# Attention, a gated mixture and a routed mixture on one core: the third weight's products of blocks 3 to 8 taken two slices at a time

## The chip, the core and the metric

The kernel runs on 1 core of one Trainium2 chip. The metric is device time in microseconds of one execution; the median of three runs of the kernel before is 960.69 us (960.13 to 963.97).

## The reference

Three layers follow each other. An attention with a local window of 32 and 32 global tokens gives 2176 rows of 512. A gated layer follows, then a routed layer of eight experts with a capacity:

```
x   = attention(q, k, v)                     # 4 x 8 heads, 512 + 32 rows, 64 wide
g   = x @ w_gate;  val = x @ w_val           # 512 -> 1536
x   = (g * sigmoid(g) * val) @ w_out         # 1536 -> 512, all of it float32
log = x @ moe2_w_gate                        # 8 logits a row; tokens assigned greedily by rank, 272 an expert
out = relu(x[mask_e] @ w1[e]) @ w2[e]        # for each expert e
```

## The kernel before, in words

The gated layer is what the change touches (the kernel calls it the first mixture). Its rows are nine **blocks** `k` = 0 to 8: blocks 0 to 7 have 256 rows, block 8 has the 128 global rows. The 1536 inner columns are twelve **slices** `f` of 128.

*One slice of one block.* `gates(f)` (line 564) multiplies the gate and the value weights with the block's inputs: 24 products in 16 bit, 12 for each half of a bank `G`. Each float32 factor is held as a high and a low part (`xth`, `xtl`; `wp` holds both parts of the weights), and three of the four combinations are added. There are two banks `G`, so slice `f + 2` writes the bank of slice `f`. After the 24 products ACT takes a tanh (L569), DVE makes `(tanh + 1) * g` (L571) and the slice's factor `th` (L573, the last reader of the bank), ACT rounds it to its high part `hh` (L576), and POOL subtracts for the low part `hl` (L578). There are three buffers of each of `hh` and `hl`.

`out(f)` (line 588) then adds the slice's product with the third weight to the block's result: `hh` with `oh` and `ol`, and `hl` with `oh`, for each of the block's two tiles of 128 rows. That is 6 products of 512 columns in a 4-byte type (3 in block 8), with `hh` and `hl` as the weights that PE loads. After slice 11, `x_rows` copies the result (`xr`, L500), and the logits follow: 8 products a tile on DVE (L523, `junk<-xr,w2gt`), put behind the gates of the next block by `logits`.

*The order of the work.* Blocks 0 to 2 run while the weights come in (`first_blocks`). `moe_block` runs blocks 3 to 8. For each slice it issues the gates, then the product of the slice before:

```
        for f in range(NF):
            yield from m.gates(f)
            ...
            if f:
                m.out(f - 1)
```

Between its pieces (`yield`) the attention of the next block is issued, piece by piece (`attn`, `globs`, `x0_t`); it ends with the transposes of L432 and the two halves `xth` (L434) and `xtl` (L435), without which the next block's gates don't go on. Blocks 5 to 8 also have the global rows' attention (`glob`, lines 443 to 480, with the split `vcl` on L307). The written order is only a wish: a planner sorts each engine's instructions by a simulated timeline before the kernel is built. `tc.add_manual_dep(..., NS, ...)` gives it a dependency that fixes an order in that timeline and makes no semaphore.

Of the kernel before, what the change touches and what calls it, by code (L numbers as in the profile page):

```python
# [13 lines left out]
OP = mybir.AluOpType  # L14
# [5 lines left out]
NF = FF // 128  # L20
# [13 lines left out]
def body(ctx, tc, units, gk, gv, wts, w2g, w1, w2, cst, cst2, out):  # L34
    nc = tc.nc
    gp, sy = nc.gpsimd, nc.sync
    NS, SY = (mybir.DependencyInfo(c, mybir.DependencyReason.DATA)
              for c in (mybir.DependencyClass.NoSync, mybir.DependencyClass.Sync))
# [19 lines left out]
    ve, sc, te = nc.vector, nc.scalar, nc.tensor  # L58
# [16 lines left out]
    def mark(ins):  # L75

        TURN[:] = [ins]
# [10 lines left out]
    def psb(tag):  # L88

        return ps.tile([128, 512], F32, name=tag, tag=tag, bufs=2 if tag == "G" else 1)  # L90
# [102 lines left out]
    def g_tile():  # L193

        return GN.pop() if GN else psb("G").rearrange("p (j t) -> p j t", j=2)
# [301 lines left out]
    def x_rows(c, px, tag):  # L497

        xr = wk.tile([128, DM], F32, name="xr", bufs=2)
        sc.activation(xr, px, AF.Copy)  # L500
        if c < 16:
            r0 = (c // 4) * 544 + 32 + 128 * (c % 4)
            sy.dma_start(xs[r0:r0 + 128, :], xr)
        else:
            sy.dma_start(xs.rearrange("(b s) d -> b s d", b=B)[:, :32, :], xr)
        if 2 * NB <= c < NT - 1:
            for e in range(NE):
                LT.append((c, e, xr))
            return
        pt = psb(tag).rearrange("p (c q) -> p c q", c=4)  # L510
        for d in range(4):
            te.transpose(pt[:, d, :], xr[:, 128 * d:128 * d + 128], ident)
        xt = wk.tile([128, 544], F32, name="pg", tag="sm")[:, :DM].rearrange("p (d t) -> p d t", d=4)
        XT_LAST[:] = [sc.activation(xt, pt, AF.Copy)]
        pl = psb(tag)
        for d in range(4):
            te.matmul(pl[:, :NE], xt[:, d], w2gc[:, d], start=(d == 0), stop=(d == 3))
        ve.tensor_copy(L[:, c], pl[:, :NE])

    def logits(n):  # L520
        for _ in range(min(n, len(LT)) if w2gt is not None else 0):
            c, e, xr = LT.pop(0)
            ve.scalar_tensor_tensor(junk[:, :DM], xr, 1.0, w2gt[:, e], op0=OP.mult, op1=OP.mult,  # L523
                                    accum_out=L[:, c, e:e + 1])

    HH = {}
# [3 lines left out]
    class Moe:  # L530
# [24 lines left out]
        def gates(self, f):  # L555
            self.scales(f)
            n, (xh, xl), ib = self.n, self.x, self.ib
            pg = g_tile()
            for j in range(2):
                i = 0  # L560
                for d in range(4):
                    o = slice(128 * d, 128 * d + 128)
                    for a, x in ((0, xh), (0, xl), (1, xh)):
                        te.matmul(pg[:, j, :n], wp_[:, f, j, a, o], x[:, d, :n], start=(i == 0), stop=(i == 11))  # L564
                        i += 1
                if j == 0:
                    yield
            th = wk.tile([128, 256], F32, name="th")
            TH[:] = [sc.activation(th[:, :n], pg[:, 0, :n], AF.Tanh, scale=ib[:, 0, f:f + 1])]  # L569
            t = th  # L570
            ve.scalar_tensor_tensor(t[:, :n], th[:, :n], 1.0, pg[:, 0, :n], op0=OP.add, op1=OP.mult)  # L571
            h = th
            mark(ve.scalar_tensor_tensor(h[:, :n], t[:, :n], ib[:, 1, f:f + 1], pg[:, 1, :n],  # L573
                                         op0=OP.mult, op1=OP.mult))
            hh = wk.tile([128, 256], F32R, name="hh", bufs=3)
            sc.activation(hh[:, :n], h[:, :n], AF.Copy)  # L576
            hl = wk.tile([128, 256], F32R, name="hl", bufs=3)
            gp.tensor_tensor(hl[:, :n], h[:, :n], hh[:, :n], op=OP.subtract)  # L578
            HH[self.k, f] = (hh, hl)

        def out(self, f):
            nt = self.n // 128
            if f == 0:
                self.px = [psb(self.tags[t]) for t in range(nt)]
            hh, hl = HH.pop((self.k, f))
            for i, (a, w) in enumerate(((hh, oh), (hh, ol), (hl, oh))):
                for t in range(nt):
                    te.matmul(self.px[t], a[:, 128 * t:128 * t + 128], w[:, f, :], start=(f == 0 and i == 0),  # L588
                              stop=(f == NF - 1 and i == 2))
            if f == NF - 1:  # L590
                for t in range(nt):
                    x_rows(2 * self.k + t, self.px[t], self.tags[t] if self.k < NB else "PTa")
# [26 lines left out]
    def moe_block(k):  # L619
        m = Moe(k)  # L620
        for f in range(NF):
            yield from m.gates(f)
            logits(f % 2)
            yield
            if f:
                m.out(f - 1)
            logits(1)
            yield
        yield
        m.out(NF - 1)  # L630


# [692 lines left out]
```

## Time and profile before

| | |
|---|---|
| median of 3 runs | 960.69 us |
| the profiled execution, its time | 965.33 us |
| its span, first to last instruction | 963.6 us |
| mean granted clock of TensorE | 0.951 |
| PE busy | 871.9 us (90%) |
| weight loads (PEld), beside PE | 732.3 us (76%) |
| DVE busy | 611.1 us (63%) |
| ACT busy | 453.0 us (47%) |
| POOL busy | 371.9 us (39%) |

The profiled execution is 4.64 us above the median. Times in the profile are microseconds from the span's start. In a timeline row the first number is the start, the second the duration; a matmul's duration holds its way through the array, so what a product costs is read from the distance between starts. A bracket gives the idle time of the engine ahead of the instruction and what ended it. The clock is the share of full speed that TensorE was granted. Blocks 3 to 8 run from 275 to 652 us; the routing and the experts follow.

### The profile page before, as it was taken

What the parts mean: (1) busy time and instruction counts of PE and PEld (TensorE: products, weight loads), DVE (VectorE), ACT (ScalarE), POOL (GpSimd) and SP (SyncE); (2) the same over time, 40 slices, a digit from 0 to 9 for tenths busy, and PEclk for the clock granted to TensorE, in tenths of its full rate; (3) what the DMA queues carried; (4) which work ended last, traced back from release to release, by engine and by line L of the source; (5) the groups of instructions that cost most, each with busy time, mean ns of one, the idle gap of its engine ahead of it and who ended that gap; (6) DMA issues with size and microseconds to landing.
All of it is one profiled execution on the core that took longest, in us unless ns stands there. A gap on an engine that the chain in (4) does not pass through costs nothing.

```text
span 963.6 us, 19509 instructions
## 1 busy us (share of the span) xinstructions
PE 871.9 (90%) x7556; PEld 732.3 (76%) x7556; DVE 611.1 (63%) x1859; ACT 453.0 (47%) x923; POOL 371.9 (39%) x344
## 2 busy tenths in 40 slices
PE   5677699999999999989979989996789989999996
PEld 4566578777788887778758757783488988999996
DVE  3677699999328579597595484268666766763210
ACT  4656454555247465445354333230554364545531
POOL 2444333444212222113111111121666786687841
PEclk8889889999999999989989999997789999999998
DMA  9631243542212233303221020001454455446600
GB/s 373 254 121 45 86 155 132 160 161 66 88 66 93 85 103 108 118 29 109 82 78 56 27 74 1 1 23 43 169 184 142 133 185 188 135 149 215 197 28 26
DMA packets 28497, 108.10 MB, mean 112 GB/s; under 512 B 3572, under 2 KB 3572, under 8 KB 28276
## 3 DMA queue, kind: packets, MB, share of 16 engines
q1 hardware_dynamic: 25332, 97.94, 30.0%
q0 software_dynamic: 3072, 8.92, 2.6%
q8 instruction: 59, 0.97, 0.4%
q14 instruction: 34, 0.28, 0.1%
HBM read 97.92 MB, written 8.91 MB: 111 GB/s over the span
## 4 chain that ended last, share of the span: by engine, by line
PE 68%; DVE 12%; issue 7%; DMA 5%; POOL 4%; ACT 3%; SPq 0%; POOLq 0%; ACTq 0%; DVEq 0%
PE G L564 26%; PE X L588 11%; PE A L1152 7%; PE A L1136 5%; PE rt L961 2%; DMA er<-w 2%; DMA xg<-xs,idx 2%; DVE junk L523 2%; DVE ge L948 1%; POOL wp L50 1%; PE PV L476 1%; PE PV L399 1%; POOL vl L50 1%; PE T L1101 1%; DMA gkr<-gv 1%
## 5 line engine op out<-in xcount | busy, mean ns | idle before, releaser
L564 PEld LDWEIGHTS <-wp 128*128 128x128 f16 x2592 | 231.6, 99 | 80.5 <-issue 52.0
L564 PE MATMUL G<-xth,wp 128*128 128x256 f16 (+1 forms) x1344 | 235.8, 270 | 4.1 <-ACT xth L434 2.5
L578 POOL TENSOR_TENSOR hl<-th,hh 128x256 fp32r<-128x256 f32 (+1 forms) x108 | 85.5, 792 | 348.1 <-ACT hh L576 274.8
L564 PE MATMUL G<-xtl,wp 128*128 128x256 f16 (+1 forms) x672 | 177.5, 270 | 4.3 <-DVE xtl L435 4.3
L1083 POOL TENSOR_TENSOR el<-er,eh 128x1024 fp32r<-128x1024 f32 x62 | 146.3, 2390 | 40.7 <-ACT eh L1080 40.4
L569 ACT ACTIVATE th<-G,ib 128x256 f32<-128x256 f32 (+1 forms) x108 | 49.4, 459 | 107.8 <-PE G L564 97.0
L571 DVE SCALAR_TENSOR_TENSOR th<-th,G 128x256 f32<-128x256 f32 (+1 forms) x108 | 43.4, 402 | 81.9 <-ACT th L569 81.0
L1080 ACT ACTIVATE eh<-er 128x1024 fp32r<-128x1024 f32 x64 | 65.5, 1054 | 49.4 <-DMA er<-w 43.2
L576 ACT ACTIVATE hh<-th 128x256 fp32r<-128x256 f32 (+1 forms) x108 | 43.4, 402 | 75.4 <-DVE th L573 75.1
L1136 PE MATMUL A<-xh,eh 128*128 128x272 f32 x256 | 77.9, 304 | 0.0
L1152 PE MATMUL A<-fh,eh 128*128 128x272 f32 x256 | 76.6, 302 | 0.0
L1136 PE MATMUL A<-xh,el 128*128 128x272 f32 x256 | 75.2, 294 | 0.0
L1136 PE MATMUL A<-xl,eh 128*128 128x272 f32 x256 | 74.9, 293 | 0.0
L1152 PE MATMUL A<-fh,el 128*128 128x272 f32 x256 | 74.4, 292 | 0.0
L1152 PE MATMUL A<-fl,eh 128*128 128x272 f32 x256 | 74.2, 291 | 0.0
L1141 DVE SCALAR_TENSOR_TENSOR fl<-A,fh 128x272 fp32r<-128x272 f32 x64 | 28.0, 439 | 59.2 <-ACT fh L1140 57.4
L523 DVE SCALAR_TENSOR_TENSOR junk<-xr,w2gt 128x512 f16<-128x512 f32 x80 | 59.0, 737 | 4.1 <-ACT xr L500 3.4
L588 PE MATMUL X<-oh,hh 128*128 128x512 f32 x156 | 57.7, 444 | 2.1 <-ACT hh L576 2.1
L588 PE MATMUL X<-oh,hl 128*128 128x512 f32 x156 | 55.7, 428 | 0.0
L573 DVE SCALAR_TENSOR_TENSOR th<-th,ib,G 128x256 f32<-128x256 f32 (+1 forms) x108 | 50.1, 464 | 2.9
L588 PE MATMUL X<-ol,hh 128*128 128x512 f32 x156 | 51.5, 403 | 0.0
L1136 PEld LDWEIGHTS A<-xl,eh 128*128 128x128 f32 x256 | 49.2, 192 | 0.1
(389 smaller groups left out, 2126.7 us busy)
## 6 DMA issues: line engine op xcount, KB each, us to landing
er<-w SPq DMA_DIRECT2D x64, 512.0 KB, 5.2
wr<-wts SPq DMA_DIRECT2D x36, 512.0 KB, 3.6
unit<-units SPq DMA_DIRECT2D x22, 688.0 KB, 4.0
unit<-gv SPq DMA_DIRECT2D x12, 640.0 KB, 3.8
wp<-units SPq DMA_DIRECT2D x10, 688.0 KB, 7.8
gkr<-gk SPq DMA_DIRECT2D x8, 608.0 KB, 4.7
xs<-xr SPq DMA_DIRECT2D x17, 256.0 KB, 2.0
gkr<-gv SPq DMA_DIRECT2D x4, 640.0 KB, 7.3
```

Of the source, the lines that this page charges most:

```text
L523: ve.scalar_tensor_tensor(junk[:, :DM], xr, 1.0, w2gt[:, e], op0=OP.mult, op1=OP.mult, accum_out=L[:, c, e:e + 1])
L564: te.matmul(pg[:, j, :n], wp_[:, f, j, a, o], x[:, d, :n], start=(i == 0), stop=(i == 11))
L569: TH[:] = [sc.activation(th[:, :n], pg[:, 0, :n], AF.Tanh, scale=ib[:, 0, f:f + 1])]
L571: ve.scalar_tensor_tensor(t[:, :n], th[:, :n], 1.0, pg[:, 0, :n], op0=OP.add, op1=OP.mult)
L573: mark(ve.scalar_tensor_tensor(h[:, :n], t[:, :n], ib[:, 1, f:f + 1], pg[:, 1, :n], op0=OP.mult, op1=OP.mult))
L576: sc.activation(hh[:, :n], h[:, :n], AF.Copy)
L578: gp.tensor_tensor(hl[:, :n], h[:, :n], hh[:, :n], op=OP.subtract)
L588: te.matmul(self.px[t], a[:, 128 * t:128 * t + 128], w[:, f, :], start=(f == 0 and i == 0), stop=(f == NF - 1 and i == 2))
L1080: q = sc.activation(h, r, AF.Copy)
L1083: q = (ve if j == 0 and i < 2 else gp).tensor_tensor(l, r, h, op=OP.subtract)
L1136: behind(te.matmul(pa_[:, :CAP], a[:, s], x[:, d], start=(i == 0), stop=(i == 11)))
L1152: behind(te.matmul(py[:, :CAP], a[:, s], x[:, f], start=(i == 0), stop=(i == 23)))
```

## The change

`moe_block` no longer issues `out(f - 1)` behind each slice's gates. Behind the gates of an even slice from 2 on it issues `out(f - 2)` and then `out(f - 1)`; slices 10 and 11 come at the block's end. `gates` also keeps the instruction that makes `hl`, and each product of `out(f - 2)` gets an order dependency on the `hl` of slice `f - 1`, so that the planner starts none of the twelve products before it has placed the last of their factors. No product, copy or transfer is added or taken away.

```
             hl = wk.tile([128, 256], F32R, name="hl", bufs=3)
-            gp.tensor_tensor(hl[:, :n], h[:, :n], hh[:, :n], op=OP.subtract)
-            HH[self.k, f] = (hh, hl)
-
-        def out(self, f):
+            q = gp.tensor_tensor(hl[:, :n], h[:, :n], hh[:, :n], op=OP.subtract)
+            HH[self.k, f] = (hh, hl, q)
+
+        def out(self, f, last=None):
+
             nt = self.n // 128
             if f == 0:
                 self.px = [psb(self.tags[t]) for t in range(nt)]
-            hh, hl = HH.pop((self.k, f))
+            hh, hl, ready = HH.pop((self.k, f))
             for i, (a, w) in enumerate(((hh, oh), (hh, ol), (hl, oh))):
                 for t in range(nt):
-                    te.matmul(self.px[t], a[:, 128 * t:128 * t + 128], w[:, f, :], start=(f == 0 and i == 0),
-                              stop=(f == NF - 1 and i == 2))
+                    q = te.matmul(self.px[t], a[:, 128 * t:128 * t + 128], w[:, f, :], start=(f == 0 and i == 0),
+                                  stop=(f == NF - 1 and i == 2))
+                    if last is not None:
+                        tc.add_manual_dep(q.ins, last.ins.name, NS, reason="all in a row")
...
             logits(f % 2)
             yield
-            if f:
+            if f and f % 2 == 0:
+                m.out(f - 2, HH[k, f - 1][2])
                 m.out(f - 1)
             logits(1)
             yield
         yield
+        m.out(NF - 2)
         m.out(NF - 1)
```

The planner sorts anew, and its order changes on PE, DVE and ACT from block 3 on. In PE's order the products with the third weight come, from block 3's first gates on, in 131 uninterrupted runs before (23, 30, 19, 20, 18 and 21 beside the gates of blocks 3 to 8) and in 70 with the change (15, 16, 11, 11, 8 and 9).

PE, block 8, where slice 2 ends and slice 3 begins (the two names after `G_` are the two banks' tiles). Before:

```order
L564 MATMUL G_7846<-xth_7399,wp_76 128x128
L588 MATMUL X0_7841<-oh_77,hh_7802 128x512
L588 MATMUL X0_7841<-ol_78,hh_7802 128x512
L588 MATMUL X0_7841<-oh_77,hl_7804 128x512
L564 LDWEIGHTS wp_76
L564 MATMUL G_7883<-xth_7399,wp_76 128x128
```

and with the change:

```order
L564 MATMUL G_7842<-xth_7399,wp_76 128x128
L564 LDWEIGHTS wp_76
L564 MATMUL G_7883<-xth_7399,wp_76 128x128
L564 LDWEIGHTS wp_76
L564 MATMUL G_7883<-xtl_7400,wp_76 128x128
```

The three products of slice 0 that stood between the two slices' gates are gone from there; they come with those of slice 1 behind the gates of slice 3.

DVE, the end of block 5, from the last step of a global piece (L480) to the second half of the next block's `xtl` (L435). Before:

```order
L480 TENSOR_SCALAR x0g<-PV,gr 32x64 x4
L523 SCALAR_TENSOR_TENSOR junk,L<-xr,w2gt 128x512
L435 TENSOR_TENSOR xtl<-PTb,xth 128x4x128
L366 ISA sm,mx<-S,mask 128x224
L366 ISA mx 128x1
L366 ISA sm,mx<-S,mask 128x224
L366 ISA mx 128x1
L307 SCALAR_TENSOR_TENSOR vcl<-unit,pscv,vch 128x1280
L523 SCALAR_TENSOR_TENSOR junk,L<-xr,w2gt 128x512
L435 TENSOR_TENSOR xtl<-PTa,xth 128x4x128
```

and with the change:

```order
L480 TENSOR_SCALAR x0g<-PV,gr 32x64 x4
L366 ISA sm,mx<-S,mask 128x224
L366 ISA mx 128x1
L366 ISA sm,mx<-S,mask 128x224
L366 ISA mx 128x1
L307 SCALAR_TENSOR_TENSOR vcl<-unit,pscv,vch 128x1280
L435 TENSOR_TENSOR xtl<-PTb,xth 128x4x128
L435 TENSOR_TENSOR xtl<-PTa,xth 128x4x128
```

Before, six of the block's sixteen logits products stand ahead of the second `xtl` at this end (two of them in these rows); with the change all sixteen stand behind it. At the end of block 6 the same count goes from four to none, and the split `vcl` stays ahead of the second `xtl` in both. At the end of block 4 it is three in both.

## Rows read from the trace of the kernel before

**Rows 1.** Page of before, part 4: the chain that ended last, by engine.

```profile
PE 68%; DVE 12%; issue 7%; DMA 5%; POOL 4%; ACT 3%; SPq 0%; POOLq 0%; ACTq 0%; DVEq 0%
```

**Rows 2.** Stretches: busy us of PE, PEld, DVE, ACT, POOL; granted clock; DMA share.

```profile
410.00:415.00 5.00, 2.43 (x17) 1.62 (x15) 4.82 (x13) 2.49 (x6) 1.14 (x1) 0.97 0.20 78
...
480.00:485.00 5.00, 3.82 (x22) 2.78 (x23) 3.49 (x17) 4.43 (x13) 0.74 (x1) 1.00 0.87 340
485.00:490.00 5.00, 3.71 (x27) 2.54 (x27) 4.82 (x16) 4.03 (x7) 1.75 (x1) 1.00 0.03 10
490.00:495.00 5.00, 2.04 (x13) 1.48 (x14) 4.97 (x14) 2.73 (x6) 1.13 (x1) 0.82 0.17 40
495.00:500.00 5.00, 5.00 (x26) 3.57 (x24) 4.80 (x14) 0.41 (x1) 0.14 (x1) 0.50 0.23 91
...
565.00:570.00 5.00, 1.96 (x10) 1.31 (x10) 4.96 (x13) 1.22 (x5) 0.00 (x0) 0.83 0.40 128
```

**Rows 3.** Timeline of PE around products with the third weight: start, duration.

```profile
597.40 0.27 PE L564 MATMUL G<-xth,wp 128*128 128x256 f16 x1
...
598.90 0.28 PE L564 MATMUL G<-xth,wp 128*128 128x256 f16 x1
...
601.86 0.27 PE L564 MATMUL G<-xth,wp 128*128 128x256 f16 x1
...
603.61 0.39 PE L564 MATMUL G<-xth,wp 128*128 128x256 f16 x2
...
603.94 0.38 PE L564 MATMUL G<-xth,wp 128*128 128x256 f16 x2
...
631.54 0.22 PE L564 MATMUL G<-xth,wp 128*128 128x128 f16 x1
...
632.36 0.23 PE L564 MATMUL G<-xth,wp 128*128 128x128 f16 x1
```

**Rows 4.** Weight loads: page of before, part 5, and the rows of line 588.

```profile
L564 PEld LDWEIGHTS <-wp 128*128 128x128 f16 x2592 | 231.6, 99 | 80.5 <-issue 52.0
...
L588 PEld LDWEIGHTS X<-oh,hh x156: 186/190/333, 122.5 to 651.5; 128*128 128x128 f32 x156
```

**Rows 5.** Timeline, end of block 5 and start of block 6.

```profile
475.81 1.16 DVE L480 TENSOR_SCALAR x0g<-PV,gr 32x64 f32<-32x64 f32 x4 [2.21 <-PE PV L476]
...
482.32 0.69 DVE L523 SCALAR_TENSOR_TENSOR junk<-xr,w2gt 128x512 f16<-128x512 f32 x1 [0.32 <-ACT xr L500]
...
493.07 0.69 DVE L523 SCALAR_TENSOR_TENSOR junk<-xr,w2gt 128x512 f16<-128x512 f32 x1
...
494.43 0.37 PE L564 MATMUL G<-xtl,wp 128*128 128x256 f16 x1 [1.60 <-DVE xtl L435]
```

**Rows 6.** Page of before, part 5: the logits' products on DVE.

```profile
L523 DVE SCALAR_TENSOR_TENSOR junk<-xr,w2gt 128x512 f16<-128x512 f32 x80 | 59.0, 737 | 4.1 <-ACT xr L500 3.4
```

**Rows 7.** Timeline, end of block 6 and start of block 7.

```profile
562.91 1.17 DVE L480 TENSOR_SCALAR x0g<-PV,gr 32x64 f32<-32x64 f32 x4 [0.28 <-PE PV L476]
...
568.42 0.37 PE L564 MATMUL G<-xtl,wp 128*128 128x256 f16 x1 [2.69 <-DVE xtl L435]
```

**Rows 8.** Timeline, block 4: factor of slice 5, start of slice 7.

```profile
376.77 0.47 DVE L573 SCALAR_TENSOR_TENSOR th<-th,ib,G 128x256 f32<-128x256 f32 x1
...
377.44 0.27 PE L564 MATMUL G<-xth,wp 128*128 128x256 f16 x1
```

**Rows 9.** Timeline, block 8: factors of slices 1 and 5, and its end.

```profile
629.86 0.34 DVE L573 SCALAR_TENSOR_TENSOR th<-th,ib,G 128x128 f32<-128x128 f32 x1
...
630.26 0.22 PE L564 MATMUL G<-xth,wp 128*128 128x128 f16 x1
...
638.59 0.34 DVE L573 SCALAR_TENSOR_TENSOR th<-th,ib,G 128x128 f32<-128x128 f32 x1
...
638.98 0.22 PE L564 MATMUL G<-xth,wp 128*128 128x128 f16 x1
...
651.55 0.50 PE L588 MATMUL X<-oh,hh 128*128 128x512 f32 x1 [0.82 <-ACT hh L576]
```

## The prediction

> **What bounds the kernel now.** I began with the chain of waits: 68% of the span hangs on PE, 12% on DVE [rows 1]. The change touches blocks 3 to 8 only, so I cut 270 to 705 us into stretches of 5 us. PE is busy throughout nearly all of them; the exceptions are the ends of blocks 4, 5 and 6, and there DVE is the full engine [rows 2]. At the end of block 5 PE is idle for 1.18, 1.29 and 2.96 us in three stretches running, then works 5 us at a clock of 0.50, 1.2 of 2.4 GHz. So two prices matter: what a product costs PE where PE is full, and what ends the wait where it is not. For the first I read PE's timeline around the moved products, for the second the timelines around the three ends, and how close the gates come to waiting for a bank.
>
> **The change, part by part.** The same 396 products of blocks 3 to 8 run, on the same data. What changes is how often PE goes from 16-bit gates to 4-byte products and back, how far the gates run ahead of DVE, and the order that the planner gives DVE.
>
> *Fewer runs.* From 597.40 to 598.90 stand one gate product and six products in one run: 1.50 us. From 601.86 to 603.61 stand three gate products and six products in two runs: 1.75 us [rows 3]. A gate product costs 0.11 us (three from 603.61 to 603.94), so the second run cost 1.75 - 0.22 - 1.50 = 0.03 us. The order has 110 runs in blocks 3 to 7 before and 61 after: 49 x 0.03 = **-1.5 us**. The bounds are nothing, and the whole difference between a 4-byte and a 16-bit weight load, 190 - 99 ns [rows 4], 49 x 0.09 = -4.5 us. I take the measured passage. The Trainium skill (TensorE: Matmul & The Clock Gate, section "Weight-path perf modes") says that the fast weight load is for 128 weights that are not FP32. The row of 190 ns beside 99 agrees; the rule alone would charge each run the difference, and this term would be -4.5 us.
>
> *Block 8.* Its gate products have 128 columns and cost 0.056 us (23 steps from 630.26 to 631.54). Three products of one slice cost 0.82 - 0.06 = 0.76 us, the last gate product taken off [rows 3, 9]; two such slices in one run save about 0.06 us each time a run goes. The order has 21 runs before and 9 after: 12 x 0.06 = -0.7 us. Against this stands the bank. DVE frees the bank of slice 1 at 629.86 + 0.34 = 630.20, and slice 3 begins at 630.26; slice 5's is free at 638.93 and slice 7 begins at 638.98 [rows 9]. Both have nothing to spare, because DVE puts two logits products of 0.74 us [rows 6] among each slice's steps. The change takes three products (0.76 us) from between slices 2 and 3, and from between 6 and 7, and DVE's order has one more logits product ahead of slice 5's factor: 0.76 + 0.76 + 0.74 = +2.3 us of waiting. At the end PE now waits 0.82 us for the last `hh`; the order has nine products (2.3 us) there to cover it, so -0.8 us. What I expect of this block is 2.3 - 0.7 - 0.8 = **+0.8 us**; the bounds are -1.5 (the waits find cover) and +2.3.
>
> *Block 4.* Here DVE is behind: slice 5's factor is done at 376.77 + 0.47 = 377.24, and slice 7's gates begin at 377.44 [rows 8]. In the new order one slice's six products (1.50 - 0.11 = 1.39 us) that stood ahead of slice 7 come after it, and sixteen logits products instead of fifteen stand ahead of slice 5's factor. The loss is 1.39 - 0.20 without the extra logits product and 1.93 with it. I take **+1.5 us**; the bounds are 0 and +3 (a second place, slice 3 to slice 5).
>
> *The end of block 5.* The chain that lets block 6 go on runs on DVE from 475.81 to 494.4 [rows 5]. Six logits products stand in it, the first at 482.32, the last at 493.07: 6 x 0.74 = 4.4 us. The new order has none. They are not gone: all sixteen now stand ahead of the factors of block 6's slices 0 to 2, and PE gets two slices ahead at most before it needs a bank. So the gain lies between 0 (all given back) and -4.4. PE is idle 5.4 us in these 15 us, then at half speed, and has two slices (5.3 us of gates) that it can do with no bank freed. I take **-2.8 us**, two thirds.
>
> *The end of block 6.* Four logits products, 3.0 us, leave the chain from 562.91 to 568.42 [rows 7], but `vcl` stays in it and waits for ACT's half, which has no cover then. Between 0 and -3.0 I take **-1.2 us**.
>
> *The end of block 4.* The wait there [rows 2] keeps its three logits products: **0**, within 1 us either way.
>
> *Other engines.* ACT, POOL and the queues issue what they issued. The third buffer of `hh` is needed for slice `f + 1` only after the pair is under way, so I cost it nothing but at the end of block 8, where the last `hh` waits for slice 8's first products, 0.5 us after the last gate product; its cover is the nine products.
>
> The sum is -1.5 + 0.8 + 1.5 - 2.8 - 1.2 = **-3.2 us**. The profiled execution would go from 965.33 to 962.1 us; it stands 4.64 us above the median, and from the median the sum gives **957.5 us**, 0.33% less.
>
> **The rivals.** *(a) The ends give all* (chance 0.17). If the logits find room behind the waits, the ends of blocks 5 and 6 give -4.4 - 3.0 = -7.4 in place of -4.0: -6.6 us in all, 954.1 us. For it speaks that DVE is only partly busy two slices after each end; against it, that it is full right behind both.
>
> *(b) Each run costs the whole weight load* (0.08). The first product's load of 190 ns can't hide behind a gate product of 0.11 us: 49 x 0.09 in place of 49 x 0.03, so -4.5 in place of -1.5, -6.2 us, 954.5 us. The passage of 0.03 us speaks against it. It is the rule of the Trainium skill named above.
>
> *(c) The gates wait for their bank* (0.15). Two gate runs now follow one another bare in every second slice. Where DVE needs longer from the last gate product to the factor than the 24 gate products between (2.6 us), PE waits up to a slice's products, 1.39 us. It decides wherever logits products stand ahead of the factor: three places in block 4 and one at the start of each of blocks 5, 6 and 7, six in all. That is 8.3 us, +0.8 in block 8, -1.5 from the runs, and the ends give nothing since their logits come back here: +7.6 us, 968.3 us. Speaking for it are the 0.20 and 0.05 us to spare [rows 8, 9]. Against it: at the start of blocks 5 to 7 PE has just waited, and DVE has had that time.
>
> *(d) All is given back* (0.15). The ends give nothing and the rest stands: -1.5 + 0.8 + 1.5 = +0.8 us, 961.5 us. That the products don't come together at all is ruled out by the order's 70 runs.
>
> **How the numbers follow.** My forecast, with its own range of 953.5 to 961, has 0.45. A measurement of this kernel can tell about 0.5% (4.8 us) from no change: faster means below 955.9, slower above 965.5. Faster are (a) and (b) for the most part and a quarter of the forecast: 0.2 + 0.11 = 0.31. Slower is most of (c), and a stretch more at half clock, worth 2.5 us as after the end of block 5 [rows 2], on (d): 0.14. The rest, 0.55, is no change. The range runs from 951.5, (a) with the better bound of block 8, to 966.5, short of (c)'s centre: about 2 in 10 stay outside.
>
> **What would show it.** Right: the second `xtl` of block 6 comes some 4 us earlier against the block's work; the logits follow it; in block 8 the gates of slices 3 and 7 wait about 0.8 and 1.5 us for L573; the last `hh` is no longer waited for; one run more or less costs 0.03 us. Wrong: waits of G for L573 in more than three places of 256 rows, or a new stretch at a clock of 0.50, or an end of block 5 that is no shorter though its logits are gone.

## The result, and the profile after

| | before | after |
|---|---|---|
| median of 6 runs each | 961.79 us | 952.69 us |
| ratio | | 0.9909 [0.9882, 0.9935] |
| ratio in a second comparison | | 0.9932 [0.9908, 0.9956] |
| profiled execution, its span | 963.6 us | 950.6 us |
| mean granted clock | 0.951 | 0.956 |

The kernel is 0.7 to 0.9% faster, 9.1 us in the first comparison. The time lies in the prediction's range (957.5 us, 951.5 to 966.5), 1.2 us above its lower edge, but the sum of -3.2 us is a third of what came, and the likeliest class, no change, was not what came.

The page of the profile after, its lines on the engines' busy time, the chain, and the logits' products:

```profile
PE 867.3 (91%) x7556; PEld 739.7 (78%) x7556; DVE 609.7 (64%) x1859; ACT 451.7 (48%) x923; POOL 373.2 (39%) x344
...
PE 65%; DVE 14%; issue 7%; DMA 5%; POOL 4%; ACT 3%; SPq 0%; POOLq 0%; ACTq 0%; DVEq 0%
...
L523 DVE SCALAR_TENSOR_TENSOR junk<-xr,w2gt 128x512 f16<-128x512 f32 x80 | 60.8, 760 | 2.7 <-ACT xr L500 2.0
```

PE's share of the chain fell from 68% to 65% [rows 1]. PE's busy time fell by 4.6 us for the same products, those of DVE, ACT and POOL moved by 1.4 at most; so what was saved is waiting, and work that had been slow. A logits product takes 760 ns on the mean where it took 737 [rows 6]: they were moved, not made cheaper. The stretches of 5 us around the three ends (busy us of PE, PEld, DVE, ACT, POOL; granted clock; DMA share):

```profile
410.00:415.00 5.00, 4.25 (x32) 2.90 (x30) 4.35 (x13) 4.42 (x9) 1.27 (x1) 1.00 0.28 105
415.00:420.00 5.00, 3.70 (x20) 3.17 (x20) 4.94 (x17) 2.51 (x6) 1.28 (x1) 0.66 0.02 5
...
480.00:485.00 5.00, 4.73 (x33) 3.36 (x32) 4.23 (x14) 4.08 (x11) 2.01 (x2) 1.00 0.13 53
485.00:490.00 5.00, 2.71 (x20) 2.09 (x19) 4.91 (x13) 4.32 (x8) 1.27 (x1) 1.00 0.40 119
490.00:495.00 5.00, 5.00 (x56) 4.52 (x55) 4.80 (x16) 1.93 (x4) 0.00 (x0) 1.00 0.33 122
495.00:500.00 5.00, 4.55 (x42) 3.90 (x39) 4.96 (x14) 2.49 (x6) 0.72 (x1) 1.00 0.00 0
...
555.00:560.00 5.00, 3.44 (x25) 2.10 (x23) 3.15 (x8) 3.31 (x5) 0.00 (x0) 1.00 0.12 26
560.00:565.00 5.00, 3.88 (x36) 3.52 (x36) 4.93 (x17) 2.08 (x6) 0.00 (x0) 1.00 0.56 207
565.00:570.00 5.00, 5.00 (x32) 2.71 (x31) 4.97 (x15) 1.04 (x3) 0.72 (x1) 1.00 0.00 0
```

Against [rows 2]: at the end of block 5 PE is idle for 0.27 and 2.29 us instead of 1.18, 1.29 and 2.96, and **the stretch at a clock of 0.50 is gone**. The end of block 6 comes earlier now, between 555 and 565: 1.56 and 1.12 us are idle there and the clock stays at 1.00, where before 3.04 us of 565 to 570 were idle at 0.83. At the end of block 4 one stretch stands at 0.66, where before one stood at 0.50:

```profile
415.00:420.00 5.00, 4.50 (x21) 3.69 (x22) 4.91 (x16) 2.96 (x6) 1.28 (x1) 0.50 0.02 5
```

The timeline of the end of block 5, as in [rows 5]:

```profile
485.23 0.86 DVE L480 TENSOR_SCALAR x0g<-PV,gr 32x64 f32<-32x64 f32 x3
...
487.18 0.37 PE L361 MATMUL S<-kk,qq 128*128 128x224 f32 x1 [1.08 <-DVE mx L366]
...
489.11 0.68 DVE L435 TENSOR_TENSOR xtl<-PTa,xth 128x512 f16<-128x512 f32 x1
...
489.34 0.62 PE L386 MATMUL PTb<-ident,pb 128*112 128x128 f32 x4 [1.22 <-DVE xtl L435]
...
490.33 0.69 DVE L523 SCALAR_TENSOR_TENSOR junk<-xr,w2gt 128x512 f16<-128x512 f32 x1
...
497.05 0.27 PE L564 MATMUL G<-xth,wp 128*128 128x256 f16 x1 [0.34 <-DVE th L573]
...
500.47 0.20 PE L399 MATMUL PV<-vh,ptl 112*128 112x65 f16 x1 [0.58 <-DVE ptl L378]
```

Before, the second `xtl` stood behind a logits product (493.07 in [rows 5]):

```profile
493.69 0.69 DVE L435 TENSOR_TENSOR xtl<-PTa,xth 128x512 f16<-128x512 f32 x1
```

The second `xtl` of block 6 starts at 489.11, 67.53 us after block 5's first tanh (421.58); before it started at 493.69, 71.52 us after that tanh (422.17): 3.99 us earlier. The logits follow it, the first at 490.33. When the logits come, one gate waits 0.34 us for its bank (497.05) and one product of the attention 0.58 us for `ptl` (500.47), which stands behind logits on DVE; before, neither waited. So they gave back 0.9 us there.

To place the rest I cut blocks 3 to 8 at the first tanh (L569) of each block; PE has done the same number of products with the third weight at each cut in both kernels, to within one. Block 8 ends at the transposes of the last `xr` (L512). Three profiles of each order (before: the first and two repeats; after: the first, the repeat, and the run with block 8 alone undone, up to block 7), in us:

| block | before | after | predicted | came |
|---|---|---|---|---|
| 3 | 64.99, 64.89, 64.90 | 65.08, 64.99, 65.06 | -0.2 | +0.1 |
| 4 | 78.68, 78.32, 78.35 | 76.55, 77.14, 75.96 | +1.1 | -1.9 |
| 5 | 77.42, 77.43, 77.43 | 71.03, 71.04, 71.07 | -3.0 | **-6.4** |
| 6 | 73.19, 72.91, 72.88 | 71.28, 73.47, 71.21 | -1.5 | -1.0 |
| 7 | 52.60, 52.59, 52.60 | 53.66, 53.98, 53.66 | -0.3 | +1.2 |
| 8 | 27.89, 27.89, 27.89 | 27.91, 27.90 | +0.8 | 0.0 |
| sum | | | -3.1 | -8.0 |

("Predicted" is the prediction's terms put into the blocks, the fewer runs at 0.03 us each; its order's 49 fewer runs are 8, 14, 8, 9 and 10.) What follows block 8, the routing and the experts, took 310.3, 306.2 and 308.9 us before and 305.1, 310.2 and 305.9 after: it differs by 4 to 5 us between executions of one order, and DVE, ACT and POOL do the same work in the same order there in both kernels, so I put none of it down to the change.

### The profile page after: what moved, and what is told of

It reads as the page before. It is cut to its first block, busy times and chain, and to the rows that moved or that the text cites. A ratio compares the mean times of both kernels' runs of the same rounds, so it can differ in the third digit from the quotient of the medians.

```text
span 950.6 us, 19510 instructions
## 1 busy us (share of the span) xinstructions
PE 867.3 (91%) x7556; PEld 739.7 (78%) x7556; DVE 609.7 (64%) x1859; ACT 451.7 (48%) x923; POOL 373.2 (39%) x344
## 4 chain that ended last, share of the span: by engine, by line
PE 65%; DVE 14%; issue 7%; DMA 5%; POOL 4%; ACT 3%; SPq 0%; POOLq 0%; ACTq 0%; DVEq 0%
PE G L564 24%; PE X L589 10%; PE A L1157 6%; PE A L1141 6%; DVE junk L523 3%; DMA er<-w 2%; DMA xg<-xs,idx 2%; PE rt L966 2%; PE PV L476 1%; POOL wp L50 1%; DVE ge L953 1%; DVE kk L348 1%; PE PV L399 1%; PE S L443 1%; POOL vl L50 1%
## 5 line engine op out<-in xcount | busy, mean ns | idle before, releaser
L564 PE MATMUL G<-xth,wp 128*128 128x256 f16 (+1 forms) x1344 | 223.5, 266 | 5.7 <-DVE th L573 3.1
L578 POOL TENSOR_TENSOR hl<-th,hh 128x256 fp32r<-128x256 f32 (+1 forms) x108 | 88.3, 817 | 334.4 <-ACT hh L576 258.5
L564 PE MATMUL G<-xtl,wp 128*128 128x256 f16 (+1 forms) x672 | 174.1, 266 | 1.8 <-DVE xtl L435 1.8
L569 ACT ACTIVATE th<-G,ib 128x256 f32<-128x256 f32 (+1 forms) x108 | 49.4, 458 | 100.3 <-PE G L564 88.3
L589 PE MATMUL X<-oh,hl 128*128 128x512 f32 x156 | 52.5, 409 | 0.0
L1141 PEld LDWEIGHTS A<-xh,eh 128*128 128x128 f32 x256 | 49.2, 192 | 0.2
```

Of the source, the lines that this page charges most:

```text
L578: q = gp.tensor_tensor(hl[:, :n], h[:, :n], hh[:, :n], op=OP.subtract)
L589: q = te.matmul(self.px[t], a[:, 128 * t:128 * t + 128], w[:, f, :], start=(f == 0 and i == 0), stop=(f == NF - 1 and i == 2))
L1141: behind(te.matmul(pa_[:, :CAP], a[:, s], x[:, d], start=(i == 0), stop=(i == 11)))
```

## The experiments

The theory after this reading, which the expectations call the logits theory and later the clock theory: at the ends of blocks 4 to 6 PE waits for a chain on DVE; each logits product in that chain costs up to its 0.74 us as idle time, and the idle time costs PE again where the work behind it runs at a clock of 0.50 [rows 2]. Its rivals: the saved runs cost more than 0.03 us each; the paired products cover the ends; the gates' banks decide.

For each kernel the table has the runs, the logits products ahead of the second `xtl` at the ends of blocks 4, 5 and 6, the time of blocks 4 to 7 in us, and for block 5 PE's idle time and the *lost clock* (stretch times one minus granted clock, summed over twentieths of the block; it also counts time in which PE is idle: of the 3.2 to 3.4 us of block 5 before, 2.6 fell on time in which PE worked). The blocks come from one profiled execution each, and some of these lie off the median of their run (before 3.5 us above it, six_more 4.0 above, held 3.6 below, b8_single 2.4 below, high_first 1.7 below); the ratios are over all executions, and differ from the ratio of the two medians by up to 0.15%.

| kernel | runs | logits ahead | block 4, 5, 6, 7 | block 5: idle, lost | ratio to before |
|---|---|---|---|---|---|
| before | 131 | 3, 6, 4 | 78.68, 77.42, 73.19, 52.60 | 5.85, 3.17 | 1 |
| before_again | 131 | 3, 6, 4 | 78.32, 77.43, 72.91, 52.59 | 5.85, 3.37 | |
| before_third | 131 | 3, 6, 4 | 78.35, 77.43, 72.88, 52.60 | 5.85, 3.41 | |
| after | 70 | 3, 0, 0 | 76.55, 71.03, 71.28, 53.66 | 2.57, 0 | 0.9909 [0.9882, 0.9935] |
| after_again | 70 | 3, 0, 0 | 77.14, 71.04, 73.47, 53.98 | 2.57, 0 | 0.9932 [0.9908, 0.9956] |
| held | 130 | 0, 0, 0 | 75.50, 72.99, 72.41, 52.73 | 3.53, 0 | 0.9936 [0.9913, 0.9958] |
| only5 | 127 | 3, 0, 0 | 78.50, 72.46, 72.88, 54.43 | 2.56, 1.70 | 0.9967 [0.9944, 0.9990] |
| no_dep | 100 | 5, 4, 4 | 78.50, 76.86, 73.16, 52.32 | 4.57, 4.96 | 0.9963 [0.9940, 0.9986] |
| together | 69 | 3, 4, 0 | 77.67, 75.66, 71.88, 52.22 | 4.73, 3.41 | 0.9964 [0.9940, 0.9987] |
| six_more | 69 | 3, 6, 4 | 78.18, 81.63, 71.48, 52.52 | 5.20, 6.82 | 0.9985 [0.9959, 1.0011] |
| b8_single | 80 | 3, 0, 0 | 75.96, 71.07, 71.21, 53.66 | 2.57, 0 | 0.9936 [0.9914, 0.9957] |
| after_held | 65 | 0, 0, 0 | 74.30, 73.73, 72.31, 52.50 | 3.40, 0 | 0.9903 [0.9870, 0.9935] |
| filler | 134 | 4, 5, 5 | 77.36, 78.73, 76.58, 52.65 | 4.69, 3.35 | 1.0012 [0.9993, 1.0031] |
| high_first | 63 | 0, 0, 0 | 74.44, 71.48, 69.18, 52.18 | 2.56, 1.68 | 0.9835 [0.9819, 0.9851] |

**The logits alone, without pairs (held).** The kernel before with

```
-        ve.tensor_tensor(l[:, :, s], pt, h[:, :, s], op=OP.subtract)
+        XTL[:] = [ve.tensor_tensor(l[:, :, s], pt, h[:, :, s], op=OP.subtract)]
...
+            tc.add_manual_dep(q.ins, XTL[0].ins.name, NS, reason="the next block's rows first")
```

where `q` is the logits product.

> The kernel before, its products unpaired, but every logits product of a block gets an order dependency on the second xtl of the next block. In the order no logits product stands ahead of the second xtl at the ends of blocks 4, 5 and 6, and the products with the third weight come in 130 runs, as before (131). The logits theory (the gain is the logits that leave DVE's chain at these ends, and the half-clock stretch that no longer follows): 7 us less than before, since only the 1.5 us of the fewer runs and the bank waits of the pairing are missing; 952 to 957 where before is 961.8. The theory of the runs (going from gates to 4-byte products and back costs 9.1 / 61 = 0.15 us a run): no change, within 1.5 us. The theory of the cover (the paired products give PE work while it waits at an end): no change, or up to 2 us less.

Measured: 5.3 us less by the medians (956.01 against 961.26), 0.64%, with one run fewer than before. In its profile block 4 gains 2.9, block 5 4.4, block 6 0.6 us, more in all than the medians give. Neither the theory of the runs nor that of the cover survives it. Its stretches at the ends of blocks 5 and 6:

```profile
485.00:490.00 5.00, 2.84 (x22) 2.31 (x23) 4.94 (x15) 3.38 (x8) 1.27 (x1) 1.00 0.30 90
490.00:495.00 5.00, 5.00 (x57) 4.57 (x55) 4.94 (x16) 1.43 (x4) 0.00 (x0) 1.00 0.25 97
555.00:560.00 5.00, 1.59 (x12) 1.06 (x11) 4.45 (x12) 2.04 (x4) 0.00 (x0) 0.74 0.39 128
560.00:565.00 5.00, 5.00 (x29) 3.64 (x27) 2.89 (x12) 1.83 (x6) 0.00 (x0) 0.58 0.14 52
```

The same kernel shows both cases: 2.16 us of idle time and a clock of 1.00 at the one end; 3.41 us in one stretch, and 0.74 and 0.58, at the other, and there only 0.6 us is left of what the logits gave. In block 5 this order does four score products (two each of L361 and L362, 0.6 us together) that the kernel before does in block 6, so its 72.99 compare as 72.4.

**Pairs in block 5 alone (only5).**

```
-            if f and f % 2 == 0:
+            if k not in (5,):
+                if f:
+                    m.out(f - 1)
+            elif f and f % 2 == 0:
```

> Pairs in block 5 alone; blocks 3, 4, 6, 7 and 8 as before. The order has 127 runs (before 131, after 70), but at the ends of blocks 5 and 6 the logits stand behind the second xtl as in the changed kernel. Logits theory: most of the gain, 6 to 8 us less than before, 954 to 956. Theory of the runs: 4 x 0.15 = 0.6 us less, no change. If the two ends give different amounts, the trace tells them apart by the mark at the start of block 6 and of block 7.

Measured: 2.5 us less by the medians (958.75 against 961.26), well under half of what the theory said. Block 5 gains 5.0, with four runs fewer in the whole kernel, so the runs are out once more. But block 6 gains 0.1 only, though no logits stand ahead there, since the clock fell (3.1 us lost); and block 7 is 1.8 us longer, of which the paragraph on together explains 1.0. And block 5 shows how little fixes the clock: over the second half of the block PE and DVE do the same work in the same order as in the changed kernel, with the same waits of 1.08 and 1.22 us at its end, and yet 1.70 us of clock are lost here and none there.

**Block 8 undone (b8_single).**

```
-            if f and f % 2 == 0:
+            if k == 8:
+                if f:
+                    m.out(f - 1)
+            elif f and f % 2 == 0:
```

> The changed kernel with block 8 as before, one slice at a time: 19 runs there in place of 9, all else in the same order. Bank theory: the waits of G for L573 in block 8 (0.86 and 0.95 us in the changed kernel) go, the last hh is waited for 0.8 us again, and ten runs more cost 0.06 us each: -1.8 + 0.8 + 0.6 = -0.4 us against the changed kernel, no change that can be measured, with the two waits gone from the trace. Theory of the runs: ten runs more cost 1.5 us, and with the last hh the kernel is 2.3 us slower than the changed one less the two waits, so 0.5 to 2.3 us slower.

Measured: 0.9936, not to be told from the changed kernel's two ratios. In the trace the two bank waits are gone (0.12 us of idle time are left ahead of the end), the last `hh` is waited for again, and block 8 takes 27.99 us (24.79 and 3.20) where the changed one takes 27.91: the parts cancel as the bank theory says, and the runs' theory asked for 0.5 to 2.3 us.

**Six DVE products put back at the end of block 5 (six_more).**

```
+        if k == 6 and t:
+            for e in range(6):
+                q = ve.scalar_tensor_tensor(junk[:, :DM], w2gt[:, e], 1.0, w2gt[:, e + 1], op0=OP.mult, op1=OP.mult,
+                                            accum_out=XTRA[:, e:e + 1])
+                tc.add_manual_dep(q.ins, XTL[0].ins.name, NS, reason="between the halves")
```

and the second `xtl` behind them.

> The changed kernel with six more DVE products of the size of a logits product (their results are not used) between the two xtl of block 6, which is where the kernel before had its logits: it puts the price of DVE's chain at the end of block 5 in alone, 69 runs. The new order also has four logits products ahead of the second xtl at the end of block 6 again, as before. Logits theory: 6 x 0.74 = 4.4 us for the end of block 5, up to 3 for the end of block 6, and 1.5 to 3 us of half clock behind the ends: 5 to 10 us slower than the changed kernel. If the end is set by something else (a transfer, ACT, the products of PE): under 2 us slower.

Measured: 961.05 us, 0.9985: the whole gain is gone, with 69 runs. In the profile block 5 alone takes 10.6 us more than in the changed kernel:

```profile
485.00:490.00 5.00, 3.72 (x25) 2.55 (x23) 4.86 (x11) 4.58 (x9) 0.97 (x1) 1.00 0.01 5
490.00:495.00 5.00, 2.40 (x10) 1.79 (x10) 4.91 (x14) 2.44 (x6) 1.26 (x1) 0.60 0.55 181
495.00:500.00 5.00, 3.95 (x24) 3.50 (x25) 4.93 (x19) 0.85 (x2) 0.00 (x0) 0.50 0.00 0
500.00:505.00 5.00, 5.00 (x27) 3.50 (x26) 4.44 (x14) 0.74 (x2) 0.00 (x0) 0.53 0.16 56
```

PE is idle for 1.28, 2.60 and 1.05 us, and the clock is 0.60, 0.50 and 0.53 in three stretches running. Idle time rose by 2.6 us (5.20 against 2.57), and 6.8 of clock are lost, 5.5 of them while PE works. The other 2.4 us of the 10.6 are work: twelve score products of L361 and L362 and the transposes and products that follow them, which the changed kernel does in block 6. So the 4.4 us of DVE cost 8.2 us here. And this profile is a costly one, 4.0 us above the run's median: by the medians the whole kernel is 7.3 us slower than b8_single of the same comparison (by the two ratios 4.7), for the six products here and the four logits products at the end of block 6, 7.4 us of DVE.

**Pairs with the logits back (together).** The trace after had shown a second thing, in block 7. The two score products of L443, which each fill 64 of a bank's 128 partitions (the trace counts them as four), stand apart there:

```profile
566.78 1.07 PE L443 MATMUL S<-gkr 128*64 128x512 f32 x2
...
567.78 0.28 PE L476 MATMUL PV<-vch,pth 128*128 128x256 f16 x1
...
568.11 1.07 PE L443 MATMUL S<-gkr 128*64 128x512 f32 x2
...
569.11 0.28 PE L476 MATMUL PV<-vch,ptl 128*128 128x256 f16 x1
```

In a row they had taken 1.01 us together before:

```profile
575.67 1.08 PE L443 MATMUL S<-gkr 128*64 128x512 f32 x4
...
576.68 0.28 PE L476 MATMUL PV<-vch,pth 128*128 128x256 f16 x1
```

Apart, each half takes 1.00 us: block 7 is longer by that. The Trainium skill (TensorEngine Tiling (Array Packing), section "Key Properties") says that different tiles of the array can work in parallel; the rows agree, for as long as nothing stands between. To put them in a row again, the score product got a dependency on the second product of L476 (`m`):

```
+                if n == 1:
+                    GVQ[:] = [m]
...
+            for d in GVQ:
+                tc.add_manual_dep(q.ins, d.ins.name, NS, reason="both in a row")
```

> The changed kernel with an order dependency that puts the two score products of L443 behind the first two products of L476, so that they stand in a row. That is worth 1.0 us in block 7 (52.6 in place of 53.7). But the new order has logits products ahead of the second xtl again, 3, 4 and 0 at the ends of blocks 4, 5 and 6 (before 3, 6 and 4, changed kernel 3, 0 and 0), with 69 runs: it is the pairing with the logits back at the end of block 5. Clock theory: block 5 takes 75 us or more in place of 71.0 and has a half-clock stretch behind its end; in all 3 to 6 us slower than the changed kernel, 956 to 959. Theory that the pairing by itself gives the time (runs, cover): 1 us less than the changed kernel.

Measured: block 7 takes 52.22 us, so the 1.0 us is there; but 4.0 us of the medians are left of the gain (962.98 against 966.99, 0.36%). Block 5 takes 75.66 us:

```profile
485.00:490.00 5.00, 1.94 (x12) 1.45 (x10) 4.82 (x15) 2.36 (x5) 0.00 (x0) 0.92 0.00 0
490.00:495.00 5.00, 3.33 (x16) 2.51 (x16) 4.88 (x14) 2.93 (x6) 1.51 (x1) 0.50 0.44 131
```

The half clock is back with four logits products, in a kernel whose products are paired as in the changed one.

**Pairs without the dependency (no_dep).** `m.out(f - 2)` in place of `m.out(f - 2, HH[k, f - 1][2])`.

> The changed kernel without the order dependency on the last factor: the pairs are only written so, and the planner has 100 runs (before 131, changed 70). Logits ahead of the second xtl: 5, 4 and 4 at the ends of blocks 4, 5 and 6. Clock theory: ends nearly as before, block 4 78 to 79 us, block 5 75 to 77, block 6 72 to 73; 31 runs fewer at 0.02 us are 0.7 us; in all 1 to 3 us less than before, 958 to 960. Theory of the runs: half of the gain, 4.6 us less than before, 956.5.

Measured: 3.6 us less than before by the medians (963.36 against 966.99), 0.37%. Blocks 4 and 6 are as before, block 5 0.6 us shorter, as the clock theory says; the medians lie nearer to the other one's 4.6, and their interval (0.14 to 0.60%) holds both. Blocks 3 to 8, where alone the orders differ, speak for the clock theory: their sum is 373.59 us against 374.77, 374.03 and 374.05, 0.4 to 1.2 less. That is one profile.

**Work for PE in the waits (filler).** The kernel before with

```
+            if f == 0 and self.k in (5, 6, 7):
+                for i in range(30):
+                    te.matmul(pg[:, 1, :n], wp_[:, 0, 0, 0, :128], PREV[0][:, 0, :n], start=True, stop=True)
```

> The kernel before with 30 products of 256 columns more ahead of the first gates of blocks 5, 6 and 7, which write a half of the G bank that the first gates overwrite; their results are not used. In the order most of them stand among the last products of the block before, where PE waits. Logits ahead of the second xtl: 4, 5 and 5. Clock theory: PE is not idle for long, so the clock stays at 1.00 behind the ends; the 8.5 us of lost clock go to under 3, and since the fillers (0.11 us each, 9.8 us in all) stand in the way here and there the kernel is 2 to 6 us faster than before. If only the idle time on the chain counts and not the clock: no gain, 0 to 4 us slower than before.

Measured: no change (1.0012), not the gain that I expected. At the end of block 4 it does what it was built for:

```profile
415.00:420.00 5.00, 3.92 (x31) 3.17 (x30) 4.86 (x17) 3.81 (x8) 1.27 (x1) 1.00 0.03 8
420.00:425.00 5.00, 5.00 (x56) 4.55 (x55) 4.90 (x16) 1.70 (x5) 0.18 (x1) 1.00 0.00 2
```

Idle time 2.64 us instead of 4.32, no lost clock, and block 4 takes 1.1 us less than the mean of before. It does 3.3 us of fillers more, and four score products (0.5 us) less, which come later. At the ends of blocks 5 and 6 the fillers went by before the long waits came: 4.69 and 3.77 us of idle time stayed, with 3.35 and 1.80 of lost clock, and the blocks grew. So it supports the clock theory in one place of three and misses in two; a filler is worth something only where the wait is.

**Both together, and the clock's luck (after_held, after_again, the two repeats of before).** after_held is the changed kernel with the logits' dependency of held.

> The changed kernel with every logits product held behind the second xtl of the next block (the order dependency of the run with the unpaired products): 65 runs, no logits product ahead of the second xtl at the ends of blocks 4, 5 and 6, where the changed kernel has 3, 0 and 0; the planner also puts the two score products of L443 in block 7 in a row again, which the changed kernel has torn apart by two products of L476. Clock theory (what an end costs is PE's idle time and, above all, the half-clock stretch that a long idle time is followed by): block 4 takes 75.5 us from first tanh to first tanh in place of 76.6, block 7 52.6 in place of 53.7, the others as in the changed kernel: 2 us less than the changed kernel, 951. If logits that are held back come up as waits of the gates for their bank: as the changed kernel or 1 to 2 us slower.

Measured: 0.9903 (956.96 against 966.99). Block 7 takes 52.50 us, as expected, and block 4 74.30, 1.2 less, but block 5 73.73 and block 6 72.31, with 3.3 us of lost clock in block 6: in all about as the changed kernel. Of the 2.7 us that block 5 is longer than in the changed kernel, 2.4 can be placed: 0.8 of idle time, 0.6 of the four score products that held also has there, and 1.0 because this order tears the score products of L443 apart in block 5:

```profile
448.24 1.07 PE L443 MATMUL S<-gkr 128*64 128x512 f32 x2 [0.22 <-DVE mx L366]
...
450.88 1.07 PE L443 MATMUL S<-gkr 128*64 128x512 f32 x2
```

No bank wait was added (four of 2.6 us in all).

> The changed kernel once more, beside the version below on the same chip. Clock theory: the same order need not meet the same clock; the end of block 4, 0.66 in one stretch of the first profile and 1.00 in the run that differs from it in block 8 alone, may fall either way, and block 4 takes 76 or 76.6 us (78 where a whole stretch is at 0.50). Blocks 5 and 6 71.0 and 71.3 with no half-clock stretch, block 7 53.7. Ratio to before 0.989 to 0.994. If the clock of 1.00 behind the ends of blocks 5 and 6 was luck, block 5 or 6 takes 73 us or more here.

Measured: block 5 again 71.04 with a clock of 1.00 behind it, but block 6 73.47:

```profile
555.00:560.00 5.00, 2.61 (x18) 1.71 (x18) 3.98 (x10) 3.64 (x6) 0.00 (x0) 0.91 0.30 96
560.00:565.00 5.00, 4.71 (x23) 3.26 (x23) 4.90 (x17) 0.72 (x4) 0.00 (x0) 0.50 0.38 137
```

The order is that of the first profile and the idle time nearly (3.63 against 3.81 us in block 6), the clock isn't. So the gain at the end of block 6 is had in two profiles of three. A miss costs 2.2 us, which is as much as the two comparisons' gains differ by; whether it is why they differ, one profile of each can't tell.

> The kernel before once more, for its clock behind the ends: the changed kernel's order has now been profiled there three times (the run with block 8 alone different among them) and lost 0, 1.7 and 1.7 us of clock at the end of block 4, none in all three at the end of block 5, and 0, 0 and 3.2 at the end of block 6. Clock theory: the kernel before loses 3 us again at the end of block 5, in every profile, since its idle time there (5.9 us) is twice that of the changed kernel; block 5 takes 76 us or more. If its half clock there was luck: block 5 takes 74 to 75 us with a clock of 1.00.

> The kernel before a third time, as in the run ahead of this one: clock theory, block 5 at 76 us or more with some 3 us of lost clock, block 6 at 72 to 74, block 4 at 78 to 79 (it had 78.7, and 78.5 in the run with pairs in block 5 alone, whose order is the same there).

Measured: 961.81 and 962.21 us (one time each, beside 961.27). Block 5 takes 77.43 us both times, with 3.4 us of lost clock. One of them:

```profile
485.00:490.00 5.00, 2.48 (x19) 1.85 (x19) 4.82 (x14) 2.71 (x5) 0.31 (x1) 1.00 0.00 0
490.00:495.00 5.00, 3.26 (x20) 2.21 (x19) 4.97 (x14) 2.73 (x6) 1.27 (x1) 0.63 0.41 129
495.00:500.00 5.00, 5.00 (x41) 3.87 (x39) 4.80 (x14) 0.48 (x1) 0.00 (x0) 0.69 0.01 2
```

The idle time falls into other stretches than in [rows 2], and the block still takes the same time to 0.01 us. So what the kernel before pays at the end of block 5 is no luck. That the changed order pays no clock there is less sure: its three profiles show none lost, only5, with the same order at that end, 1.70 us.

**A version that beats both (high_first).** As after_held, and in the first half of slice 0 of blocks 4 to 8 the products with `xth` come ahead of those that need `xtl`:

```
+                terms = [(d, a, x) for d in range(4) for a, x in ((0, xh), (0, xl), (1, xh))]
+                if f == 0 and j == 0 and self.k > NB:
+                    terms.sort(key=lambda z: z[2] is xl)
+                for d, a, x in terms:
```

> The changed kernel with the logits held behind the second xtl (as in an earlier run) and, in blocks 4 to 8, the first half of slice 0's gates in another order: the eight products with xth first, then the four with xtl. In the order PE has nine gate products ahead of the first that needs xtl, where it had two: 7 x 0.11 = 0.8 us of work in each wait for xtl at the ends of blocks 4, 5 and 6. If that wait is what ends last: idle time falls by up to 0.8 us an end, 2 us in all against the version without it (which was 0.97% under before), and the clock falls less: 1.1 to 1.4% under before. If the scores and transposes that stood behind the two products on PE (S and T of the block after next) are now late: no gain.

Measured: 949.64 us against 965.52, 1.65% [1.49, 1.81] under before, more than I expected. The end of block 6, after_held:

```profile
557.80 0.38 PE L565 MATMUL G<-xth,wp 128*128 128x256 f16 x2 [0.81 <-ACT xth L434]
...
560.12 0.37 PE L565 MATMUL G<-xtl,wp 128*128 128x256 f16 x1 [1.94 <-DVE xtl L435]
```

and high_first:

```profile
554.28 1.14 PE L567 MATMUL G<-xth,wp 128*128 128x256 f16 x9 [0.81 <-ACT xth L434]
...
556.60 0.60 PE L567 MATMUL G<-xtl,wp 128*128 128x256 f16 x4 [1.18 <-DVE xtl L435]
```

The wait for `xtl` fell from 1.94 to 1.18 us, by the 0.8 us of the seven products put ahead; and the clock, which had fallen in after_held (3.3 us lost in block 6), stayed at 1.00: block 6 takes 69.18 us, 3.1 less. There the 0.8 us came with four times itself. That it kept the clock is not shown, since one profile of each stands against the other; at the end of block 5, where idle time also fell by 0.8 us, the clock went the other way (1.68 us lost, none in after_held). The gain of the whole kernel rests on five executions. Without the pairs this order was not tried.

## Why the prediction was right in direction and too small

**The end of block 5, -2.8: the step that failed.** Its mechanism was right: the logits left the chain, the second `xtl` came 3.99 us earlier, and 0.9 us was given back in block 6. As idle time it was well sized, 5.85 - 2.57 = 3.3 us for the -2.8. What the step left out is the clock. It said that PE "then" works "at half speed", had the 0.82 and 0.50 in its rows, and counted 2.5 us for such a stretch as a risk of the rival that gives all back; that the stretch would *go* was in no term. 3.2 to 3.4 us of clock were lost before in each of three profiles, 2.6 of them while PE worked, and none after in three. Block 5 less its idle time and less the clock lost while PE worked is 69.0 us in the three profiles of before, 68.5 in the three of after, and 68.3 to 68.4 in only5, together and no_dep: 3.3 of idle time, 2.6 of clock and 0.5 of shorter work make the 6.4 us. (In held, 69.5, after_held, 70.3, six_more, 70.9, and filler, 71.1, work was moved into the block, or torn apart there, or added; high_first's 67.2 is not explained.)

The Trainium skill (TensorE: Matmul & The Clock Gate, section "HAM oscillation — how this bites in real kernels") says that a long wait of PE is paid a second time by the work behind it, which starts at 1.2 GHz. Block 5 before agrees in the second payment, 3.2 to 3.4 us lost behind 5.85 us idle, but not in the one long wait: the longest there is 1.60 us [rows 5].

**The end of block 6, -1.2.** The waits at the end itself fell by 1.5 us (4.2 to 2.7), a little more than said, which is two logits products. Of the four that the prediction counted in the chain from 562.91 to 568.42 only two stand in it: the other two start at 561.20 and 561.93, and DVE then waits 0.28 us for PE [rows 7], so they cost nothing there. The block's idle time fell by 0.4 us only, since 0.9 us came back at its start. The lost clock, 1.7 to 1.9 us before, was 0 in two profiles and 3.2 in the third.

**The end of block 4, 0.** Three logits stayed, and yet the block is 1.9 us shorter in spite of 0.9 us of new bank waits. The block's other idle time fell by about 1.2 us (all of it from 4.36 to 4.08 on the mean of three profiles each, with those 0.9 in the second); in the first two profiles the wait of a score product (L361) for `mx` at the end went from 2.53 to 1.30 us. The lost clock, 3.4, 1.7 and 1.7 us before, was 1.7, 1.7 and 0. Why that wait is shorter was not tested.

**The bank waits, +1.5 in block 4 and +2.3 in block 8.** They came, and smaller:

```profile
359.59 0.27 PE L564 MATMUL G<-xth,wp 128*128 128x256 f16 x1 [0.42 <-DVE th L573]
...
376.71 0.27 PE L564 MATMUL G<-xth,wp 128*128 128x256 f16 x1 [0.51 <-DVE th L573]
...
622.53 0.22 PE L564 MATMUL G<-xth,wp 128*128 128x128 f16 x1 [0.86 <-DVE th L573]
...
632.01 0.22 PE L564 MATMUL G<-xth,wp 128*128 128x128 f16 x1 [0.95 <-DVE th L573]
```

Block 4 waits 0.51 us at slice 7, where predicted, and 0.42 at slice 4. Block 8 waits 0.86 us at slice 3, and 0.95 at slice 7, where 1.5 was expected. With one in block 3 (0.44 us at 313.77) and one at the start of block 6 that is four places of 256 rows, 1.7 us. By the prediction's own sign (more than three is wrong) this step's count was low; its price, 0.9 instead of 1.5, was high. Rival (c), 8.3 us in six places, is refuted.

**The runs, -1.5 and -0.7.** Two slices in block 7 after, one run of twelve products:

```profile
605.51 0.28 PE L564 MATMUL G<-xth,wp 128*128 128x256 f16 x1
...
613.55 0.28 PE L564 MATMUL G<-xth,wp 128*128 128x256 f16 x1
```

and before, four runs of two and four:

```profile
610.31 0.71 PE L588 MATMUL X<-oh,hh 128*128 128x512 f32 x2
...
618.42 0.71 PE L588 MATMUL X<-oh,hh 128*128 128x512 f32 x2
```

8.04 against 8.11 us for the same 60 products: 0.07 / 3 = 0.02 us a run, 1.0 us for 49. The price of the whole weight load, 0.09 us a run, is refuted for these blocks, and rival (b) with it. In block 8, whose gate products are half as long, full-speed work fell from 26.4 to 25.4 us (27.89 less 0.82 for `hh` and 0.70 for `xr`; 27.91 less 1.81 and 0.69): 0.08 us a run, -1.0 where -0.7 was said. The last `hh` is no longer waited for. So block 8 came to 0.0 instead of +0.8.

**Not in the prediction: block 7, +1.2.** The planner tore the two score products apart, 1.0 us. I had read the new order on PE for the products with the third weight and on DVE for the logits, not for the other products that it moved.

Rival (a) gave the nearest number (954.1), by idle time that did not all come; rival (d) is refuted by block 5. That the range holds the time is in part luck: its lower edge is rival (a) with a block 8 in which the waits find cover (954.1 - 0.8 - 1.5 = 951.8, not 951.5), and neither came, while the clock, which did, is in no bound on that side.

**Open.** Why the clock falls behind one end and not behind another with the same order and idle time (block 6 after: 3.81, 3.77 and 3.63 us idle; 0, 0 and 3.2 lost; the end of block 5 in after and in only5) is not shown here. So of the gain in blocks 3 to 8, the idle time is the change's, the clock at the end of block 5 is so in all three profiles of its order, and the clock in blocks 4 and 6 is what these few profiles happened to get.

## What to carry to other kernels

Where PE waits for another engine and the rows behind the wait show a clock of 0.50, a step on that engine has two prices: its own time, and the half-speed stretch that goes or comes with it. Count both, in both directions, the second as a range that begins at nothing: a microsecond of DVE put back cost 1.9 in a costly profile (8.2 for 4.4), and 0.6 to 1 by the whole kernel's times (4.7 to 7.3 for 7.4). Before pairing anything, hold what nobody waits for (the logits) behind what somebody does (`xtl`), and put work that needs only the early half ahead of the wait; here these two, on top of the pairs, took the gain from 0.7 to 0.9% to 1.65%, though with the logits held alone it stood at 0.97%, no clear step. And read the whole of a planner's new order on the engine that is full.

## What was not expected of the hardware

- Two score products of half a bank each take 1.01 us in a row and 1.00 us *each* with other products between (two in block 7, fourteen in block 5 of after_held).
- The same order with the same idle time (3.8 and 3.6 us in block 6) had a clock of 1.00 behind it in one profile and of 0.50 in another, which made 2.2 us. The same order at the end of block 5, with waits of 1.08 and 1.22 us in both kernels, lost no clock in three profiles and 1.70 us in a fourth.
- A change from gates to 4-byte products and back costs 0.02 us beside gates of 256 columns and 0.08 beside gates of 128, far under the 0.09 between the two weight loads in the first case, and near it in the second.
